# Attention and two MLPs on one core: p·v in two slices instead of four, and the copies of the remaining transposes on ScalarE

## The chip, the core and the metric

The program runs on one core of a Trainium2 chip. The metric is the device time of one execution in microseconds; the time before is the median of 3 runs. The engines are called TensorE (PE in the rows; PEld is its weight load), VectorE (DVE), ScalarE (ACT), GpSimd (POOL) and SyncE (SP, which issues the DMAs).

## The reference

For 4 batches of 8 heads, 576 positions and 64 numbers a head, q and k are turned by a rotary table, softmax attention is taken, and the result goes through two MLPs of width 512 and 2048.

```python
q_rot, k_rot = (rotate(q), rotate(k))
scores = (1.0 / np.sqrt(D)) * np.matmul(q_rot, k_rot.transpose(0, 1, 3, 2))
scores = scores - np.max(scores, axis=-1, keepdims=True)
attn = np.exp(scores)
attn = attn / (np.sum(attn, axis=-1, keepdims=True) + 1e-09)
attn_out = np.matmul(attn, v)
...
h = x @ w_in      # first MLP: 0 below -1, h above 1, (h + 1)**2 / 4 between
x = g @ w_out
...
h = x @ w_in      # second MLP: g = s * max(h, 0)**2 + b
out = g @ w_out
```

## The kernel before

**Units.** Two heads make a pair; 4 batches give 16 pairs. A pair is 9 units: four blocks of 128 query rows for each of the two heads, and one unit for the 64 rows left over from both. Units are numbered n = 0 to 143; the first batch is n = 0 to 35. For each unit `qk` computes the scores `sc` in PSUM on TensorE (L353), VectorE takes the negated row maximum `nm` (L355), and ScalarE the exponential `p` with its row sums (L360). `sc` has two buffers, so the scores of a unit can begin when the exponential of the unit two before has read its own.

**Transposes.** Two units later `tmain` transposes four 128-column blocks of `p` into a PSUM bank `tp` (L375) and copies the bank to `pt`: ScalarE for head 0 and the middle unit (L380, L378), VectorE for head 1 (L382). The last 64 columns of `p` remain. When the units of a group are through, `trem` transposes them (L388, L391) into `tr`, and a copy takes them to `ptr` (L393). A pair has two groups: g = 0 with 320 query rows and g = 1 with 256.

**Products and scaling.** `av` multiplies the transposed `p` by `v`: four key blocks `kt`, each for two heads (L401, two rows of the profile for each product), and then the remaining columns out of `ptr` (L406, L408). These products have 64 columns of weights (128*64 in the rows), the others 128. `inverse` takes the reciprocal of the row sums (L416), which GpSimd spreads into `eb` (L418, one buffer). `finish` runs the products in slices, then transposes `eb` on TensorE into `rm` (L429, L431), copies `rm` to `r` on ScalarE (L434), and multiplies on VectorE (L437 to L440).

**Order.** For n < 48 (`NS`) `finish` yields after each slice, and each slice is issued with the transposes of one unit, beginning three units after the group's last (`LS`). From n = 48 all four blocks go at once, and work of the first MLP fills in between (`run_fill`, L180). GpSimd has the rotary products of the next pair (`qin`, `kin`, L96), and from about 57 us also parts of the weights' conversion (`wm`, `w`). Within the attention a scheduler puts each engine's instructions in order from its own estimate of times, so an edit in one place moves rows on every engine. From about 440 us on, TensorE's order is the order of the code.

Of the kernel before, what the change touches and what calls it, by code (L numbers as in the profile page):

```python
# [24 lines left out]
NP = H // 2  # L25
# [31 lines left out]
NS = 48  # L57
PARK_AT = range(96, 144, 6)
LS = 3
SLICES = [[0], [1], [2], [3]]  # L60
SPLITX = 1
N1 = 288
N7 = 480
# [3 lines left out]
def kernel(ctx, tc, qq, kk, vv, tab, ww1, ww2, s, b, out):  # L67
    nc = tc.nc
# [180 lines left out]
    def bank(name):  # L249
        return ps_b.tile([P, 512], F32, tag="bank", name=name)  # L250
# [86 lines left out]
    pt = {}  # L337
# [46 lines left out]
    def trem(i, g):  # L384

        tp = bank("tr")
        for n in range(2):
            nc.tensor.transpose(tp[:, n * P:(n + 1) * P], p_t.pop((i, 2 * g + n))[:, 512:640], ident)  # L388
        m = 256
        if g == 0:  # L390
            nc.tensor.transpose(tp[:, 256:384], p_t.pop((i, 4))[:, 512:640], ident)  # L391
            m = 384
        nc.vector.tensor_copy(pt["r", g][:, :m], tp[:, :m])  # L393

    def av(i, g, ps, kts):

# [24 lines left out]
    def finish(i, g, e, eb, slices):  # L421
        ps = bank("av")
        for kts in slices:
            av(i, g, ps, kts)
            if 3 not in kts:
                yield
        rm = bank("rm")
        for t in range(2):
            nc.tensor.transpose(rm[:, t * P:(t + 1) * P], eb[:, 2 * t:2 * t + 2, :].rearrange("p j d -> p (j d)"), ident)  # L429
        if g == 0:  # L430
            nc.tensor.transpose(rm[:, 256:384], e[:, 4:5].to_broadcast([P, P]), ident)  # L431
            u_t[i] = att2.tile([P, S], F32, tag="u", name="u")
        r = att2.tile([P, 384], F32, tag="r", name="r", bufs=1)
        nc.scalar.copy(r[:, :384 - 128 * g], rm[:, :384 - 128 * g])  # L434
        u = u_t[i]
        c = slice(256 * g, 256 * g + 256)
        nc.vector.tensor_tensor(out=u[:, c], in0=ps[:, :256], in1=r[:, :256], op=ALU.mult)  # L437
        if g == 0:
            nc.vector.tensor_tensor(out=u[:D, 512:], in0=ps[:D, 256:320], in1=r[:D, 256:320], op=ALU.mult)
            nc.vector.tensor_tensor(out=u[D:, 512:], in0=ps[D:, 256:320], in1=r[D:, 320:384], op=ALU.mult)  # L440
            return
        bb, hp = divmod(i, NP)
        nc.sync.dma_start(out=xd[hp, :, bb * S:(bb + 1) * S], in_=u_t.pop(i))
# [155 lines left out]
    def do_t(n):  # L599
        if LT <= n < len(units) + LT:  # L600
            i, k = units[n - LT]
            tmain(i, k)
            if k in (4, 8):
                trem(i, k // 8)
                rbs[i, k // 8] = inverse(i, k // 8)
# [3 lines left out]
    def do_av(n):  # L609
        late = LS if n < NS else LA  # L610
        for m in range(n - LS if n < NS else n - LA - (n == NS), n - late + 1):
# [3 lines left out]
            if k in (4, 8) and (i, k // 8) in rbs:  # L615
                todo.append((i, k, finish(i, k // 8, *rbs.pop((i, k // 8)), SLICES if n < NS else [range(4)])))
        while todo:
# [561 lines left out]
```

## Time and profile before

| | |
|---|---|
| median of 3 runs | 1115.1 us (1114.06 to 1116.26) |
| the profiled execution | 1114.57 us |
| its span | 1112.8 us |
| TensorE busy | 1074.0 us, 97% of the span |
| VectorE, ScalarE, GpSimd busy | 778.2, 628.5, 431.1 us |
| granted clock | 1.00 over the whole span |

A busy TensorE need not be at its peak: a matmul's row may cover time in which it only passes through, and rows overlap. What the engine's work needs is read from the distance of the starts, or from the chain of work.

### The profile page before, as it was taken

To read this page: it belongs to the slowest core of one execution; us is meant where nothing else is said; L and a number is where in the kernel's file an instruction comes from. 1 tells how busy PE (TensorE), PEld (TensorE's weight loads), DVE (VectorE), ACT (ScalarE), POOL (GpSimd) and SP (SyncE) were. 2 spreads that over 40 slices of the span, in tenths; PEclk is the share of its full clock that TensorE was granted. 3 is DMA by queue.
4 is the path that set the end of the run, shared out by engine and by line. 5 is a ranking of instruction groups with operands and counts; after the bars stand their busy time and mean duration, and the time that the engine had idled before them with its cause. 6 is when DMAs were issued, how large, how long until landed. Compare 5 with 4: busy or idle time off the path is not lost.

```text
span 1112.8 us, 20049 instructions
## 1 busy us (share of the span) xinstructions
PE 1074.0 (97%) x7296; PEld 982.0 (88%) x7296; DVE 778.2 (70%) x1449; ACT 628.5 (56%) x1430; POOL 431.1 (39%) x564
## 2 busy tenths in 40 slices
PE   3999999989999999999999999999999999999998
PEld 3776788877898889999999999999999999999997
DVE  6899988778667653454756667866787778677754
ACT  4777777767666665454545455474555448334431
POOL 7989978686563322432535345110212110000000
PEclk9999999999999999999999999999999999999999
DMA  7665856756675544646465663231322843221221
GB/s 219 172 206 162 260 177 194 226 158 193 195 230 181 159 143 152 224 160 201 136 197 202 212 231 129 67 122 50 124 79 90 313 162 114 83 85 40 81 63 36
DMA packets 109762, 173.24 MB, mean 156 GB/s; under 512 B 29408, under 2 KB 80608, under 8 KB 109664
## 3 DMA queue, kind: packets, MB, share of 16 engines
q1 hardware_dynamic: 109664, 171.97, 48.7%
q8 instruction: 57, 0.93, 0.4%
q14 instruction: 41, 0.34, 0.1%
HBM read 110.10 MB, written 48.56 MB: 143 GB/s over the span
## 4 chain that ended last, share of the span: by engine, by line
PE 82%; DVE 7%; DMA 3%; ACT 3%; POOL 3%; issue 2%; SPq 0%; POOLq 0%; ACTq 0%; DVEq 0%
PE hps L180 15%; PE sum L915 14%; PE yps L831 6%; PE yps L830 6%; PE yps L829 6%; PE y L180 5%; PE sc L353 5%; PE yps L765 4%; PE av L401 4%; PE yps L767 4%; PE yps L766 4%; PE h L180 4%; PE tp L375 3%; DVE nm L355 2%; ACT p L360 1%
## 5 line engine op out<-in xcount | busy, mean ns | idle before, releaser
L180 PE MATMUL hps<-xh,w 128*128 128x288 f32 (+4 forms) x640 | 163.4, 324 | 0.0
L360 ACT ACTIVATE p<-sc,nm 128x576 f32<-128x576 f32 x144 | 106.7, 743 | 32.1 <-DVE nm L355 29.5
L353 PE MATMUL sc<-kh,qs 128*128 128x288 f32 x336 | 103.5, 331 | 22.0 <-DVE qs L307 12.3
L355 DVE TENSOR_REDUCE nm<-sc 128x1 f32<-128x576 f32 x144 | 106.7, 749 | 22.6 <-PE sc L353 21.9
L923 ACT ACTIVATE four<-four,b_sb,s_sb 128x480 f32<-128x480 f32 x64 | 47.4, 783 | 126.3 <-DVE four L922 126.3
L831 PE MATMUL yps<-gh,w 128*128 128x480 f32 (+1 forms) x320 | 118.5, 370 | 0.0
L829 PE MATMUL yps<-gh,w 128*128 128x480 f32 (+1 forms) x320 | 118.4, 370 | 0.0
L830 PE MATMUL yps<-gl,w 128*128 128x480 f32 (+1 forms) x320 | 118.4, 370 | 0.0
L96 POOL TENSOR_TENSOR wm<-wm,w 128x256 f32<-128x256 f32 x80 | 70.0, 896 | 119.1 <-ACT w L138 62.2
L180 PEld LDWEIGHTS hps<-xh,w 128*128 128x128 f32 x640 | 113.3, 188 | 1.0
L180 PE MATMUL hps<-xl,w 128*128 128x288 f32 (+4 forms) x320 | 103.7, 324 | 0.0
L353 PEld LDWEIGHTS sc<-kh,qs 128*128 128x128 f32 x336 | 64.5, 195 | 41.7 <-ACT p L360 20.2
L375 PE MATMUL tp<-ident,p 128*128 128x128 f32 x576 | 88.3, 278 | 6.8 <-ACT p L360 3.3
L353 PE MATMUL sc<-kz,qs 128*128 128x288 f32 x336 | 94.5, 303 | 0.0
L765 PE MATMUL yps<-gh,w 128*128 128x288 f32 (+3 forms) x288 | 93.2, 324 | 1.1 <-ACT ys L503 0.5
L766 PE MATMUL yps<-gl,w 128*128 128x288 f32 (+3 forms) x288 | 92.8, 322 | 0.0
L767 PE MATMUL yps<-gh,w 128*128 128x288 f32 (+3 forms) x288 | 92.8, 322 | 0.0
L96 POOL TENSOR_TENSOR wm<-wm,raw 128x256 f32<-128x256 f32 x16 | 12.8, 819 | 176.5 <-ACT raw L138 176.5
L375 PEld LDWEIGHTS tp<-ident,p 128*128 128x128 f32 x576 | 70.8, 143 | 10.2 <-ACT p L360 3.7
L180 PE MATMUL y<-gh,w 128*128 128x288 f32 x320 | 74.2, 302 | 2.0 <-DVE ptr L393 0.9
L401 PE MATMUL av<-pt,vin 128*64 128x256 f32 (+1 forms) x512 | 75.7, 417 | 0.0
L106 DVE TENSOR_TENSOR gl<-hps,gh 128x288 fp32r<-128x288 f32 (+4 forms) x88 | 46.5, 528 | 40.5 <-ACT gh L102 40.4
(154 smaller groups left out, 2910.3 us busy)
## 6 DMA issues: line engine op xcount, KB each, us to landing
wraw<-in_ww SPq DMA_DIRECT2D x56, 512.0 KB, 4.2
w<-parkd SPq DMA_DIRECT2D x24, 512.0 KB, 6.1
kin<-in_k SPq DMA_DIRECT2D x15, 576.0 KB, 4.8
qin<-in_q SPq DMA_DIRECT2D x15, 576.0 KB, 4.2
kh<-kin SPq DMA_DIRECT2D x60, 144.0 KB, 2.7
parkd<-wraw SPq DMA_DIRECT2D x16, 512.0 KB, 3.3
xs<-y1d SPq DMA_DIRECT2D x32, 240.0 KB, 2.6
xd<-u SPq DMA_DIRECT2D x16, 288.0 KB, 2.7
```

What stands on the lines that cost most here:

```text
L180: m = nc.tensor.matmul(out_ps, l, r, start=(i == 0), stop=(i == n - 1))
L353: nc.tensor.matmul(sc[:, half, o:o + n], l, r[:, k0:k0 + n], start=m == 0, stop=m == len(todo) - 1)
L355: maxs[i * 9 + k] = nc.vector.tensor_reduce(out=nm, in_=sc[:, :, :288], axis=AX.XY, op=ALU.max, negate=True).ins
L375: m = nc.tensor.transpose(v[:, c, :], p[:, c * P:(c + 1) * P], ident)
L401: nc.tensor.matmul(ps[j * D:(j + 1) * D, :n], v[:, kt, j, :], pt[g][:, kt, j, :], start=kt == 0, stop=False)
L765: nc.tensor.matmul(acc, wh, gh, start=f == 0, stop=False)
L766: nc.tensor.matmul(acc, wh, gl, start=False, stop=False)
L767: nc.tensor.matmul(acc, wl, gh, start=False, stop=last)
L829: nc.tensor.matmul(acc, wh, gh, start=f == 0, stop=False)
L830: nc.tensor.matmul(acc, wh, gl, start=False, stop=False)
L831: nc.tensor.matmul(acc, wl, gh, start=False, stop=last)
L915: nc.tensor.matmul(acc, l, r, start=j == 0, stop=j == len(t) - 1)
```

## The change

Each group of the first 48 units now runs its products in two slices of two key blocks, so the last slice stands two units earlier; and for the four pairs of the first batch (i < `NP`, which is 4) ScalarE copies `tr` to `ptr`, not VectorE.

```diff
-SLICES = [[0], [1], [2], [3]]
+SLICES = [[0, 1], [2, 3]]
...
-        nc.vector.tensor_copy(pt["r", g][:, :m], tp[:, :m])
+        (nc.scalar.copy if i < NP else nc.vector.tensor_copy)(pt["r", g][:, :m], tp[:, :m])
```

On TensorE, at the first group of the first pair, from the transposes ahead of its first slice, there stood before (x2 are the two heads of one key block):

```order
L375 MATMUL tp<-ident,p 128x128 x4
L401 MATMUL av<-pt,vin 64x320 x2
L353 MATMUL sc<-kh,qs_107 128x288
L353 MATMUL sc<-kz_109,qs_107 128x288
L353 MATMUL sc<-kh,qs_107 128x288
L353 MATMUL sc<-kz_109,qs_107 128x288
L375 MATMUL tp<-ident,p 128x128 x4
L401 MATMUL av<-pt,vin 64x320 x2
```

and there stands now:

```order
L375 MATMUL tp<-ident,p 128x128 x4
L401 MATMUL av<-pt,vin 64x320 x4
L353 MATMUL sc<-kh,qs_107 128x288
L353 MATMUL sc<-kz_109,qs_107 128x288
L353 MATMUL sc<-kh,qs_107 128x288
L353 MATMUL sc<-kz_109,qs_107 128x288
L375 MATMUL tp<-ident,p 128x128 x4
L401 MATMUL av<-pt,vin 64x320 x4
L406 MATMUL av<-ptr,vin 64x64 x2
L408 MATMUL av<-ptr,vin 64x256 x2
L429 MATMUL rm<-ident,eb 128x128 x2
```

Four products follow each other where two did, and the remaining products and the `rm` transposes come after the second slice instead of the fourth. Over the whole program TensorE goes over from other work to products of 64 weight columns 61 times before and 43 times now.

On ScalarE, in the third group (pair 1, first group), the copy now stands behind that of the middle unit (`pt` of L378):

```order
L360 ACTIVATE p,sums<-sc,nm 128x576
L378 COPY pt<-tp 128x8x64
L393 COPY ptr<-tr 128x384
L306 ACTIVATE qs_108<-qin 64x576
L360 ACTIVATE p,sums<-sc,nm 128x576
```

So a copy and the scaling of `qs` lie there between two exponentials.

On GpSimd, the ninth group's `eb` (pair 4, first group) stood before in this place, behind the memset of `vin`:

```order
L96 TENSOR_TENSOR w<-wm,wa 128x256 x2
L96 TENSOR_TENSOR kin<-kin,tab_sb 128x2x144 x4
L274 MEMSET vin 64x64
L418 COPY eb<-sume 128x256
L96 TENSOR_TENSOR kin<-kin 128x288
```

and now it stands here:

```order
L96 TENSOR_TENSOR kin<-kin,tab_sb 128x2x144 x2
L96 TENSOR_TENSOR wm<-wm,w 128x256 x2
L274 MEMSET vin 64x64
L96 TENSOR_TENSOR kin<-kin 128x288 x2
L418 COPY eb<-sume 128x256
```

Two pieces of `wm` and two of `kin` are now ahead of it. The `eb` of the fifth group came behind one more piece of `kin` and one of `w`, that of the seventh behind one more piece of `kin`.

## Rows read from the trace of the kernel before

**Rows 1.** Windows: length; busy PE, PEld, DVE, ACT, POOL; clock, DMA share, GB/s.
```profile
25.13:52.65 27.52, 27.52 (x185) 21.45 (x184) 23.62 (x38) 21.11 (x50) 26.35 (x33) 1.00 0.62 173
52.65:75.00 22.35, 21.85 (x159) 15.49 (x158) 21.15 (x34) 17.39 (x42) 19.54 (x25) 1.00 0.61 172
75.00:92.00 17.00, 16.85 (x125) 11.73 (x123) 15.21 (x27) 12.99 (x31) 14.20 (x19) 1.00 0.63 189
92.00:130.00 38.00, 34.91 (x254) 25.28 (x254) 36.04 (x60) 29.34 (x71) 35.37 (x46) 1.00 0.76 227
55.79:74.14 18.35, 18.35 (x136) 13.22 (x135) 17.24 (x30) 13.93 (x34) 15.86 (x21) 1.00 0.61 178
```

**Rows 2.** TensorE's waits, 130 to 450: first and last of ten (us, times, longest).
```profile
PE sc L353 <- ACT p L360: 3.9, 6, 1.4
...
PE tr L388 <- ACT ys L503: 0.3, 1, 0.3
```

**Rows 3.** TensorE's waits, 450 to the end: first of two rows.
```profile
PE yps L765 <- ACT ys L503: 0.5, 1, 0.5
```

**Rows 4.** Chain that ended last, 30 to 53: start, us, what.
```profile
36.56 0.69 PE av L401 x4
37.25 0.72 PE sc L353 x4
...
41.32 0.53 PE sc L353 x4
41.85 0.58 PE av L401 x4
```

**Rows 5.** The same chain, 128 to 200.
```profile
184.43 2.30 PE av L401 x16
...
197.06 1.88 PE av L401 x16
```

**Rows 6.** Lines by form, 25.13 to 92: count, busy us, mean ns, idle before.
```profile
L393 DVE COPY ptr<-tr 128x384 f32<-128x384 f32 x4 | 2.2, 546 | 0.0
...
L434 ACT COPY r<-rm 128x384 f32<-128x384 f32 x3 | 1.4, 480 | 0.7 <-PE rm L431 0.7
...
L393 DVE COPY ptr<-tr 128x256 f32<-128x256 f32 x3 | 1.2, 414 | 0.0
...
L434 ACT COPY r<-rm 128x256 f32<-128x256 f32 x3 | 1.1, 366 | 0.2 <-PE rm L429 0.2
```

**Rows 7.** Timeline of GpSimd: start, us, instruction.
```profile
70.92 0.39 POOL L418 COPY eb<-sume 128x256 f32<-128x256 f32 x1
...
83.20 1.92 POOL L96 TENSOR_TENSOR wm<-wm,w 128x256 f32<-128x256 f32 x2
...
89.57 0.85 POOL L418 COPY eb<-sume 128x256 f32<-128x256 f32 x1
...
107.76 0.39 POOL L418 COPY eb<-sume 128x256 f32<-128x256 f32 x1
```

**Rows 8.** Timeline of TensorE, the rm transposes of three groups.
```profile
76.41 0.44 PE L429 MATMUL rm<-ident,eb 128*128 128x128 f32 x2
...
94.89 0.44 PE L429 MATMUL rm<-ident,eb 128*128 128x128 f32 x2
...
115.00 0.44 PE L429 MATMUL rm<-ident,eb 128*128 128x128 f32 x2
```

**Rows 9.** GpSimd's waits, 25.13 to 92.
```profile
POOL qin L96 <- DMA qin<-in_q: 3.0, 2, 2.4
POOL eb L418 <- PE rm L429: 2.6, 2, 2.4
```

**Rows 10.** Timeline of ScalarE: a PSUM copy and two exponentials.
```profile
68.25 0.60 ACT L378 COPY pt<-tp 128x512 f32<-128x512 f32 x1
68.73 0.77 ACT L360 ACTIVATE p<-sc,nm 128x576 f32<-128x576 f32 x1
...
87.50 0.74 ACT L360 ACTIVATE p<-sc,nm 128x576 f32<-128x576 f32 x1 [0.63 <-DVE nm L355]
```

## The prediction

> **What bounds the kernel now.** I read the windows by stage first, because the edit touches the first 48 units alone, which are through at about 120 us. After 25 us TensorE is nearly always busy: 27.52 of 27.52 us, 21.85 of 22.35 and 16.85 of 17.00 [rows 1]. That is 66.22 of 66.87 us, with VectorE at 59.98, ScalarE at 51.49 and GpSimd at 60.09. From 92 to 130 it turns round: VectorE is busy for 36.04 of 38.00 us, and TensorE stands for 3.1. A busy TensorE can hide waits, so I then read the chain of work from 30 to 53 us: it runs on TensorE from row to row, transposes, products, scores [rows 4]. For the later stages I read the waits of TensorE: the largest from 130 to 450 us is 3.9 us, the smallest shown 0.3, and all ten add up to 11.7 [rows 2]; from 450 us to the end the two together are 0.9 [rows 3]. So an early microsecond won on TensorE should still be there at the end, because behind it TensorE goes on nearly without a gap.
>
> **Breaks on TensorE, removed.** Going over to the products and back costs time. Four rows of products take 0.69 us and sixteen in one piece 2.30 [rows 4, 5], so a row inside costs (2.30 - 0.69)/12 = 0.134 us and the entry 0.69 - 4 x 0.134 = 0.15. For 256 columns 0.58 and 1.88 give 0.108 a row and again 0.15. Scores behind products take 0.72 us, behind transposes 0.53 [rows 4], so the way back costs 0.19. A break is thus worth 0.34 us. The order on TensorE has 18 fewer of them over the program. Two go in each group, and the first six groups, which lie whole before 92 us, lose twelve: 12 x 0.34 = 4.1 us. The others fall after 92 us, where TensorE waits for VectorE anyway; I give them nothing, and at most 6 x 0.34 = 2.0 more.
>
> **Copies off VectorE.** From 25 to 92 us there are seven of the eight copies, four of 546 ns and three of 414 [rows 6], 3.4 us together. Does the first term need them? After it the stretch would last 66.87 - 4.1 = 62.8 us. VectorE without the copies has 59.98 - 3.4 = 56.6 to do, 90% of it, the share that it has now (59.98/66.87). With them it would be at 96%. So the second edit adds nothing of its own to the sum: it lets the first arrive. Without it, at a share of 90%, the stretch could not shorten at all, and at 96% by the whole 4.1 us; halfway is 2 us.
>
> **Copies onto ScalarE.** ScalarE's copies of the same shapes out of PSUM, those of `r`, take 480 and 366 ns [rows 6]. Eight copies are 4 x 0.48 + 4 x 0.37 = 3.4 us more on an engine with 15.4 us idle in the stretch. The price is what stands behind one in the queue: an exponential, and behind that TensorE's next scores. In one place the exponential starts without a wait behind the copy of `pt` (68.25, then 68.73), and there a further copy delays it in full; at 87.50 it waited 0.63 us for the maximum, and there the copy hides [rows 10]. Between nothing and 3.4 us I take a quarter, 0.8, since about half stand in such a place and TensorE has other work ready for part of that.
>
> **`rm` two units earlier.** A unit takes 18.35/9 = 2.04 us [rows 1], so TensorE now wants `eb` 4.1 us earlier, and everything behind `rm` in its queue (the scores of the next unit) waits if GpSimd has it not ready. Margins now: fifth group, `eb` done at 70.92 + 0.39 = 71.31, `rm` at 76.41, so 5.1 us; seventh 94.89 - 90.42 = 4.5; ninth 115.00 - 108.15 = 6.85 [rows 7, 8]. Take off 4.1, and the pieces that the new order puts ahead of `eb`: 0.96 us each by the `wm` rows (1.92 for two) [rows 7], two for the fifth group, one for the seventh, four for the ninth. That leaves -0.9, -0.6 and -1.1 us. Against this GpSimd itself waited 2.6 us for `rm` of the group before, since `eb` has one buffer [rows 9], and gets that back. I charge 0.9 us for one such wait; the ends are nothing and, with ten groups at 1 us, 10 us.
>
> **GpSimd as a lid.** It was busy for 60.09 us of 66.87. Of the 6.8 idle us 2.6 go, as just said. If the other 4.2 (3.0 of them for the loading of `qin` [rows 9]) stay as they are, it cannot pass the stretch under 64.3 us, so that 2.6 us is the most the stretch can gain, where the other terms give 4.1 - 0.8 - 0.9 = 2.4. The two agree nearly, and I keep 2.4.
>
> **Behind 130 us** the scheduler puts rows in another order on all engines, though the work is the same. I set this at nothing; its bounds are about half of the 11.7 us of waits either way.
>
> **Sum.** 1114.57 - 2.4 = 1112.2 us for the profiled execution. It is 0.5 us under the median of the three runs, so against that median I forecast 1115.1 - 2.4 = **1112.7 us**. What a measurement here tells from no change is about 0.2%, 2.2 us, so the forecast lies just beyond that edge.
>
> **Rivals.**
> - *VectorE alone is the bound, and breaks are worth nothing.* For it: GpSimd and VectorE share the load closely, and from 55.79 to 74.14 TensorE's weight load is busy for only 13.22 of 18.35 us, 72%, while VectorE is at 94% [rows 1]. Then only the copies behind 52.65 us count, two of 546 and three of 414 ns, 2.3 us, less the 0.8 and 0.9 from above: 1114.5 us, no change. Against it: the same window has TensorE busy for all of its 18.35 us, and the starts in the chain show no gap for what would be headroom. The Trainium skill (Perfetto Trace Analysis, "Identifying the Most-Contended Engine") says to judge TensorE by its weight load's share and not by its matmuls' busy time, and by that rule VectorE would be the engine to relieve, and the breaks would give nothing. The chain [rows 4] does not bear it out. Chance 0.2.
> - *`eb` comes late, and TensorE stands.* GpSimd's in-order queue at 90% is what speaks for it. It makes the kernel slower than before by over 2.2 us once the ten groups lose 4.1 - 0.8 + 2.2 = 5.5 us, 0.55 us each. At 0.8 us each, 8 us in all, the sum is +4.7: 1119.8 us. Against it: the first, third, fourth, sixth and eighth groups keep more room, and TensorE's order puts some `rm` behind the next scores. Chance 0.1.
> - *The later order is worse.* If the waits between 130 and 450 us grow by 5 us, the time is 1117.7. Nothing in the profile speaks for it but that every engine's order changes. Chance 0.1.
> - *Everything fits.* GpSimd's loads come earlier too, the copies hide, and the last groups' breaks or the later order give some 2 us: 1115.1 - 6 = 1109 us. Chance 0.12.
>
> **Numbers.** The forecast's own case, a gain of 1.3 to 4 us, has 0.48, and about two thirds of it lie beyond 2.2 us. Faster: 0.32 + 0.12 = 0.44. The same: 0.16 and the first rival's 0.2, 0.36 together. Slower: the second and third, 0.2. For 8 in 10 the range goes from the case where everything fits, 1109, to the third rival, 1117.7, and leaves out the late `eb` in its dear form and some of what lies below. Its own range for the likeliest case is 1111 to 1114.
>
> **What would show it.** Right: the same units pass from 25 to 92 us in 64 to 65 us, products stand as eight rows in the chain with one entry, TensorE stays nearly gapless there, and from 450 us on all is shifted by one amount. Wrong: TensorE's waits show `rm` behind GpSimd; waits of the scores for the exponential grow by more than a microsecond; VectorE's idle time grows by what the copies gave back; or the shift at 130 us is gone by 450, which would put the cause into the later order.

## The result, and the profile after

The changed kernel takes 1120.85 us (median of 5 runs, 1119.31 to 1122.18), the kernel before beside it 1115.25 (1114.06 to 1116.26): a ratio of 1.0051 [1.0038, 1.0064], 5.6 us slower. The forecast was 1112.7 us with a range up to 1117.7. The profiled execution took 1119.31 us, its span 1117.5, 4.7 more than before.

The windows of the changed kernel over the same stretches as [rows 1] (length; busy PE, PEld, DVE, ACT, POOL; clock, DMA share, GB/s):

```profile
25.13:52.65 27.52, 24.64 (x180) 18.58 (x179) 21.81 (x33) 20.82 (x51) 23.82 (x31) 1.00 0.64 178
52.65:75.00 22.35, 18.86 (x146) 14.46 (x148) 17.75 (x27) 16.54 (x40) 20.03 (x26) 1.00 0.55 153
75.00:92.00 17.00, 15.96 (x122) 12.05 (x118) 14.22 (x26) 12.93 (x32) 13.22 (x19) 1.00 0.69 198
92.00:130.00 38.00, 32.43 (x243) 24.67 (x242) 34.53 (x56) 28.23 (x68) 33.61 (x42) 1.00 0.71 206
```

TensorE was busy for 66.22 of 66.87 us from 25 to 92; now it is for 59.46. But VectorE is less busy too (53.78 where it was 59.98), and so are the other two: nobody took the room. What TensorE waits for shows it. First its waits from 25 to 130 us in the kernel before, then in the changed kernel (us, times, longest):

```profile
PE sc L353 <- ACT p L360: 3.6, 5, 1.2
```

```profile
PE sc L353 <- ACT p L360: 11.7, 13, 2.4
PE av L401 <- DVE pt L382: 1.2, 2, 0.6
```

The scores wait for the exponential that has to read their buffer first, that of the unit two before: 8 us more. Behind 130 us the list adds up to 12.0 us over nine rows against 11.7 [rows 2], and from 450 us on one row of 0.5 is left [rows 3]:

```profile
PE sc L353 <- ACT p L360: 5.5, 8, 1.5
PE y L180 <- DVE gl L106: 1.5, 2, 1.1
...
```

To compare the same work and not the same clock time, I cut windows by units: from the start of the exponential of unit 2 to that of unit 50, in three pieces of 16 units, and read the sum line. Before, then after:

```profile
sum 101.86, PE 98.40 PEld 71.85 DVE 93.31 ACT 77.87 POOL 91.29; mean PE 32.80 PEld 23.95 DVE 31.10 ACT 25.96 POOL 30.43
```

```profile
sum 106.64, PE 93.23 PEld 70.70 DVE 90.19 ACT 80.30 POOL 91.00; mean PE 31.08 PEld 23.57 DVE 30.06 ACT 26.77 POOL 30.33
```

TensorE's busy time fell by 5.2 us, and its idle time rose from 3.5 to 13.4, at a granted clock of 1.00 in all pieces of both. The three pieces got 3.8, 0.5 and 0.5 us longer; in the second and third TensorE is busy for 2.3 and 2.7 us less, and idle for 2.9 and 3.2 more.

The following table is the tool for all that comes: the start of a unit's exponential in ScalarE's timeline, less the same start in the kernel before (us). The versions are explained with the experiments. Unit 4 shows what is only the beginning of the program; units 48 to 66 what the attention of the first units brought; 140 is behind all of the first MLP's filling. Each row is one profiled execution, which need not be the typical one: that of "products halved" took 2.1 us more than the median of its kernel, that of "room on VectorE, four" 1.9.

| kernel | 4 | 16 | 18 | 36 | 48 | 50 | 66 | 84 | 104 | 140 |
|---|---|---|---|---|---|---|---|---|---|---|
| changed | -0.7 | -0.3 | +3.1 | +4.9 | +3.1 | +4.1 | +5.3 | +6.3 | +5.9 | +5.9 |
| slices only | -0.5 | -0.2 | +2.7 | +5.2 | +6.4 | +6.5 | +7.1 | +12.4 | +9.6 | +10.0 |
| copies only | -0.3 | -1.1 | -1.0 | -1.1 | -1.7 | -1.8 | -1.7 | -1.8 | -0.1 | -0.1 |
| k load first | -0.4 | -0.0 | +1.2 | +7.4 | +5.2 | +4.3 | +12.9 | +17.0 | +13.9 | +14.0 |
| k load behind v | -0.5 | -0.6 | -1.4 | +3.8 | +4.3 | +2.7 | +4.8 | +9.0 | +9.1 | +9.4 |
| two slices, spread | -0.4 | -1.0 | -0.2 | +3.5 | +2.8 | +1.2 | +3.2 | +2.8 | +2.9 | +3.0 |
| three slices | -0.5 | -1.3 | -0.4 | +0.6 | +2.1 | +1.4 | +4.4 | +4.9 | +1.0 | +5.0 |
| code order, four | +0.7 | +1.8 | +1.7 | +5.1 | +3.5 | +3.0 | +17.8 | +21.6 | +18.9 | +24.1 |
| code order, two | +0.8 | -0.1 | +2.9 | +4.7 | +3.3 | +3.7 | +17.5 | +18.5 | +16.9 | +20.4 |
| room on VectorE, four | -0.7 | -0.7 | -0.7 | -0.6 | -2.1 | -4.1 | -0.1 | +3.1 | +2.9 | +3.0 |
| room on VectorE, two | -0.3 | +0.0 | +3.5 | +4.4 | +2.4 | +0.9 | +2.0 | +5.5 | +1.6 | +1.7 |
| room on VectorE, spread | -0.3 | -1.5 | -1.2 | +0.7 | -2.8 | -2.3 | -1.3 | +3.1 | -2.1 | -2.0 |
| rm apart, copies | -0.5 | -1.2 | -1.0 | -1.1 | -1.0 | -1.9 | -1.6 | +5.7 | +5.9 | +6.0 |
| one head left out | -0.6 | -0.6 | -0.6 | -0.9 | -2.6 | -3.7 | -1.7 | +10.3 | +7.9 | +8.0 |
| one head left out, two | -0.5 | -0.7 | +0.8 | +5.4 | +5.1 | +4.9 | +5.8 | +11.3 | +10.1 | +10.3 |
| products halved | -0.4 | -1.1 | -1.4 | -2.2 | -5.2 | -6.5 | -6.9 | +5.1 | +6.8 | +6.9 |
| k not multiplied, four | -1.3 | -2.5 | -2.7 | +0.3 | -1.1 | -1.8 | +0.8 | +1.5 | -1.4 | +1.9 |
| k not multiplied, two | -1.8 | +0.3 | +1.5 | +7.9 | +6.4 | +7.8 | +10.5 | +16.0 | +14.7 | +14.7 |
| both | -1.3 | -2.9 | -2.8 | -0.2 | -1.0 | -2.3 | -1.5 | +1.5 | +2.3 | +2.4 |

The changed kernel loses 3.4 us between units 16 and 18, holds that with some swing to unit 48, and has 4.1 at unit 50. At 130 us, between units 52 and 53 of the kernel before, the shift is 4.2 to 4.8 us. It goes up to 5.9 by unit 104, 1.2 us of that come back by 630 us for a reason that stays open, and the end is 4.7 us late. So the loss arises before 130 us; what comes behind moves it to and fro.

**The step at unit 18.** The chain of work that ended last, in the changed kernel:

```profile
40.95 0.61 DVE pt L382
...
41.60 1.08 PE av L401 x6
42.67 0.73 PE sc L353 x4
43.41 0.44 PE tp L375 x4
43.84 1.01 PE av L401 x8
...
45.33 0.60 SPq L268
...
48.03 0.53 SPq L443
...
48.67 5.06 DMA kin<-in_k
...
53.94 3.66 POOL kin L96 x5
...
58.25 0.80 POOL kin L96
...
59.08 0.67 ACT kin L318
59.75 0.74 ACT p L360 x2
...
60.53 0.81 PE sc L353 x4
```

The products are through earlier, which frees a buffer of `vin`, so SyncE's queue now has the loads of the third pair's v ahead of the fifth pair's k. In SyncE's own timeline, before and then after:

```profile
46.07 0.33 SPq L261 DMA_DIRECT2D kin<-in_k  x1
48.28 1.95 SPq L268 DMA_DIRECT2D vin<-in_v  x3
```

```profile
45.33 2.61 SPq L268 DMA_DIRECT2D vin<-in_v  x4
48.03 0.53 SPq L443 DMA_DIRECT2D xd<-u  x1
48.67 0.43 SPq L261 DMA_DIRECT2D kin<-in_k  x1
```

The load goes out 2.6 us later, GpSimd waits for it, ScalarE's conversion of `kin` waits for GpSimd, and the exponential stands behind that conversion in ScalarE's queue. No row of the prediction was about SyncE.

### The profile page after: what moved, and what is told of

It is laid out like the page before. It is cut to its first block, busy times and chain, and to the rows that moved or that the text cites. A ratio compares the mean times of both kernels' runs of the same rounds, so it can differ in the third digit from the quotient of the medians.

```text
span 1117.5 us, 20060 instructions
## 1 busy us (share of the span) xinstructions
PE 1070.3 (96%) x7296; PEld 983.4 (88%) x7296; DVE 776.3 (69%) x1441; ACT 631.2 (56%) x1438; POOL 430.3 (39%) x564
## 4 chain that ended last, share of the span: by engine, by line
PE 79%; DVE 7%; DMA 5%; POOL 3%; ACT 3%; issue 2%; SPq 1%; POOLq 0%; ACTq 0%; DVEq 0%
PE hps L180 15%; PE sum L915 13%; PE yps L831 6%; PE yps L830 6%; PE yps L829 6%; PE sc L353 4%; PE yps L765 4%; PE y L180 4%; PE yps L767 4%; PE yps L766 4%; PE h L180 4%; PE av L401 3%; PE tp L375 3%; DMA qin<-in_q 1%; POOL qin L96 1%
## 5 line engine op out<-in xcount | busy, mean ns | idle before, releaser
L180 PE MATMUL h<-xh,w 128*128 128x288 f32 x320 | 72.0, 301 | 4.1 <-ACT ys L503 1.1
```

The costliest lines, as they stand in the source:

```text
L180: m = nc.tensor.matmul(out_ps, l, r, start=(i == 0), stop=(i == n - 1))
```

## The experiments

The theories, as they came up. **Queue (Q):** the k load behind the v loads is the loss. **Bursts (B):** two heavy units with four products each are followed by two or three light ones without; with two score buffers TensorE cannot work ahead in the light ones, so it idles there for what it saved in the heavy ones. **Copies (C):** the copies on ScalarE delay exponentials. **Order:** every edit shifts rows on all engines, and the kernel before lies well. Later also **VectorE as a lid** and **GpSimd as a lid**.

### First: the parts, and the queue

Slices only (the copies back on VectorE) and copies only (`SLICES` as before) undo one half of the diff each. The other two force the order on SyncE:

```diff
# k load first: the changed kernel, with the v loads of pair 2 behind the k load of pair 4
...
+                if n == 20:
+                    load_qk(4, "q")
+                    with tc.issue_after(load_qk(4, "k")):
+                        load_v(2)
# k load behind v: the kernel before
...
-                    load_qk(i + 2, "q" if k == 4 else "k")
+                    with tc.issue_after(vdma[2]) if (i, k) == (2, 6) else ExitStack():
+                        load_qk(i + 2, "q" if k == 4 else "k")
```

Slices only: 

> Two slices, but the copies of the remaining transposes stay on VectorE. Theory Q (the queue): with products done earlier, SyncE's order puts the loads of v ahead of a later pair's load of k; that load comes some 3 us late, GpSimd waits for it, a cast on ScalarE waits for GpSimd, and the exponential behind it and TensorE's scores wait too. The order of this kernel has the loads of v ahead as the changed kernel has, so Q expects +3 to +6 us against the kernel before. Theory B (bursts): eight products in a row hold up the next scores, and with two score buffers the lighter units in between can't make up for it; it expects +3 to +6 us too. Theory C (the copies on ScalarE delay the exponentials): no copies are moved, so -1 to +1 us.

Copies only: 

> Four slices as before, the copies of the first batch on ScalarE. The order of SyncE is the same as before, that of TensorE nearly. Q and B expect -1.5 to +1 us against the kernel before; C expects +3 to +6 us.

k load first: 

> The changed kernel (two slices, copies on ScalarE), with one order forced on SyncE: the fifth pair's load of k stands ahead of the third pair's loads of v, as it did in the kernel before. Q expects the step at the 18th unit to go, and +1 to +3 us against the kernel before instead of +5.6. B and C expect +4.5 to +6 us, since the slices and the copies are those of the changed kernel.

k load behind v: 

> The kernel before (four slices, copies on VectorE), with the opposite order forced on SyncE: the fifth pair's load of k stands behind the third pair's loads of v, as in the changed kernel. Q expects +2 to +4 us against the kernel before, with GpSimd waiting for that load; less if the scheduler, which knows of the order, moves the cast on ScalarE out of the way. B and C expect -1 to +1 us.

Measured: slices only 1123.45 us, ratio 1.0076 [1.0060, 1.0092]; copies only 1114.15, 0.9987 [0.9977, 0.9997]; k load first 1129.28, 1.0125 [1.0107, 1.0144]; k load behind v 1122.54, 1.0068 [1.0053, 1.0084].

The slices cost, the copies do not: C has fallen. Slices only, k load first and k load behind v all lie outside what any theory had expected, on the slow side. Copies only is the one version which leaves no work out that is faster than the kernel before, by 1.4 us, barely more than its interval. It was 1.5 us ahead up to unit 84 (-1.8, less the -0.3 of the beginning) and lost that between units 84 and 104; its windows there:

```profile
230.00:235.00 5.00, 3.44 (x17) 3.21 (x18) 3.95 (x10) 3.91 (x11) 5.00 (x9) 0.69 0.31 105
235.00:240.00 5.00, 5.00 (x28) 4.98 (x27) 1.68 (x4) 3.69 (x9) 3.48 (x4) 0.62 0.11 30
```

Of Q the place is right and the sum wrong. With the k load forced behind the v loads, GpSimd waits 6.7 us in one place (for the transfer of `kin` to `kh`), and the kernel before loses 5.2 us between units 18 and 36. Put ahead of them, it takes the step at unit 18 down from 3.4 to 1.2 us, and the kernel then loses 6.2 between units 18 and 36. So the step is real, but it is not all that the change costs. Part of the losses behind it can be the clock's: behind the v loads it was 0.50 from 66 to 68 us, with the k load first from 71 to 73, in slices only from 110 to 113; the changed kernel had 1.00 throughout these units.

### Second: the bursts by themselves

```diff
-SLICES = [[0, 1], [2, 3]]
+SLICES = [[0, 1], [], [2, 3]]        (two slices, spread)
+SLICES = [[0, 1], [2], [3]]          (three slices)
-M1 = False
+M1 = True                            (TensorE in code order; four slices, and two)
```

Spread and three slices keep the copies on ScalarE, and in both the k load stands ahead of the v loads. In code order, TensorE's rows stand as the program has them, and not as the scheduler put them.

Spread: 

> The changed kernel with an empty slice between its two slices, so that a unit with four products is followed by one without, and the rm transposes come one unit later. The order of the engines keeps the fifth pair's k load ahead of the third pair's v loads, as in the kernel before. Bursts (TensorE cannot run ahead of two score buffers, so it idles in a unit without products what it lost in one with four): the unit without products now lies between the two heavy ones, and part of the lulls goes; with the queue's 3 us gone as well, 1114 to 1117 us, the exponential of unit 20 within 1 us of the kernel before, and TensorE's waits for ACT p from 25 to 130 us at 5 to 9 us. Order (any edit here moves the rows of all engines, and the kernel before had a lucky order): 1118 to 1124 us, with the loss in steps at places that have nothing to do with the units of four products. No theory makes it faster than 1113 us.

Three: 

> The changed kernel with three slices: four products in the first unit, two in each of the next two; one break less a group than before instead of two. The k load stays ahead of the v loads here too. Bursts: the load is smoother than in two slices; half of the break savings (2 us of 4) are at stake and half of the lulls come with them, 1114 to 1117 us. Order: 1118 to 1124 us, in steps that lie elsewhere.

Code order, four slices: 

> The kernel before with TensorE in the order of the code from the first instruction on, where the scheduler chose it before; the other engines are still scheduled. It is there as the partner of the next. All theories: 1125 to 1190 us, since the filling work of the first MLP stands where the code put it.

Code order, two slices: 

> The changed kernel with TensorE in the order of the code, so that against its partner TensorE's order differs in the slices alone. The k load is behind the v loads here as in the changed kernel. Bursts: against its partner the first 16 units gain nothing although 0.34 us a break are saved, TensorE's waits for ACT p grow by as much as the breaks gave, and with the queue's step at unit 18 it is 2 to 6 us slower than its partner. Order: with TensorE's order fixed the breaks saved (4 us) come through, at most the queue's 3 us go against them, and it is within 2 us of its partner or faster.

Measured: spread 1116.86 us, ratio 1.0019 [1.0010, 1.0028]; three slices 1118.90, 1.0034 [1.0022, 1.0047]; code order 1135.33 with four slices and 1137.42 with two (ranges 1134.91 to 1140.57 and 1133.29 to 1138.90, so no difference).

At unit 48 the versions stand as the bunching would have it: copies only -1.7, three slices +2.1, spread +2.8, the changed kernel +3.1. But this last has the queue's step of 3.4 us in it, and without it the order would be another. TensorE's idle time between units 2 and 50 is 2.5, 7.6, 7.4 and 13.4 us in these four. The pair in code order fits less well: two slices are 1.8 us ahead of four at unit 16, where B wanted nothing, lose 3.0 at the queue's step, win 1.4 again, and are level at unit 48 (-0.2). By the whole time the pair fits Order's expectation (within 2 us, or faster), but TensorE's waits for exponentials from 25 to 130 us grew as B wanted, from 6.4 to 11.8 us. The whole time of three slices lies where Order wanted it, beyond B's range; 2.9 us of that arose between units 48 and 140.

TensorE's timelines show the bursts more directly. Take its idle time between units 2 and 50, behind the first product, and count what follows twelve or more rows of scores and transposes without a product, so a light stretch. In the kernel before that is 0.8 us, in the changed kernel 10.1 us in ten places, 2.4 of them at the queue's step. In all seven kernels of this document with two slices it is 8.2 to 13.6 us, in all ten with four at most 1.8; three slices have 5.7, spread 4.9 (1.6 with room on VectorE). In code order, where the scheduler has no hand in TensorE's rows, it is 0.0 us with four slices and 9.7 with two. So this idle time comes with the slices, whatever the order. One such place in the changed kernel, on TensorE, then on VectorE:

```profile
107.65 0.60 PE L375 MATMUL tp<-ident,p 128*128 128x128 f32 x4
109.81 0.40 PE L353 MATMUL sc<-kh,qs 128*128 128x288 f32 x1 [1.55 <-ACT p L360]
```

```profile
106.93 0.41 DVE L437 TENSOR_TENSOR u<-av,r 128x256 f32<-128x256 f32 x1
107.26 0.96 DVE L137 SCALAR_TENSOR_TENSOR wa<-wraw,wa 128x512 f32<-128x512 uint16 x1
108.14 0.75 DVE L355 TENSOR_REDUCE nm<-sc 128x1 f32<-128x576 f32 x1
```

Here the exponential waits for its maximum, and VectorE comes to that without a pause from the scaling and a conversion. In four of the ten places, 5.6 us together, the exponential waited for a maximum before which VectorE had no pause: part of the light units' slowness is VectorE's queue.

### Third: room on VectorE

```diff
+            if lean[0]:
+                nc.scalar.copy(hi, a)
+                pool_tt(out=m, in0=a, in1=hi, op=ALU.subtract)
+                pool_tt(out=lo, in0=m, in1=a, op=ALU.add)
+                return
```

These kernels leave out VectorE's part (L134 to L137) of the weights' conversions, so those weights are not right; `lean` holds for the conversions that the first 51 steps issue. A fourth version goes the other way from two slices: four slices, the copies on ScalarE, and `rm` in a step of its own.

Four slices: 

> The kernel before, with the four VectorE instructions (wm and wa, L134 to L137) of the weights' conversions left out that the attention's first 51 steps issue; so the values of those weights are not computed rightly, and GpSimd and ScalarE keep their part. VectorE has some 15 us less to do between 55 and 130 us. It is the partner of the next two. If VectorE is the lid behind 55 us, unit 48 starts 3 to 8 us earlier than in the kernel before; if GpSimd or the order of rows is, 0 to 2 us. In all 1104 to 1115 us.

Two slices: 

> The changed kernel with the same VectorE instructions left out. Its k load is still behind the v loads. VectorE as a lid (it has to be fed all the time from 55 us on, and a lull in TensorE's bursts is lost for good): with room on VectorE the loss against its partner shrinks from 3 to 5 us at units 36 and 48 to between 0 and 2, and what is left is the queue's step at unit 18. Order (every edit shifts rows, and the kernel before lies well by luck): the loss stays at 3 to 7 us.

Two slices, spread: 

> The version with an empty slice between the two, with the same VectorE instructions left out; its k load is ahead of the v loads. VectorE as a lid: the savings of the breaks come through now, and at units 36 and 48 it is 1 to 4 us ahead of its partner, where with the conversions it was 3.5 and 2.8 us behind. Order: it stays 2 to 4 us behind.

rm apart: 

> Four slices as before, the copies on ScalarE, and the rm transposes in a step of their own one unit after the fourth slice, so that the heaviest unit gets lighter: the opposite way to two slices. If bursts on TensorE and the feeding of VectorE are the cause, it is at or under the version with the copies alone (1114.2): 1111 to 1114 us. Order: 1114 to 1121 us.

Measured: 1115.83, 1114.32 and 1111.78 us (ratios 1.0010 [1.0000, 1.0020], 0.9997 [0.9986, 1.0007], 0.9972 [0.9960, 0.9983]); rm apart 1121.41, 1.0066 [1.0047, 1.0084].

By the whole times VectorE as a lid looks confirmed; by the units it is one in the last piece alone. With 14 us less on VectorE between units 2 and 50 (78.96 against 93.31) the partner with four slices starts unit 48 2.1 us earlier than the kernel before (0.7 of it already at unit 4), and unit 50 4.1 us earlier. The pieces from unit 18 to 34 and from 34 to 50, in the kernel before and then in this partner:

```profile
56.57:89.27 32.70, 32.55 (x243) 23.53 (x242) 29.83 (x52) 24.91 (x59) 27.31 (x35) 1.00 0.63 189
89.27:125.70 36.43, 34.06 (x248) 24.21 (x245) 34.74 (x56) 27.77 (x67) 33.88 (x44) 1.00 0.73 214
```

```profile
55.88:88.52 32.64, 32.48 (x243) 23.46 (x242) 24.82 (x44) 26.02 (x62) 25.69 (x36) 1.00 0.64 201
88.52:121.61 33.09, 32.32 (x239) 22.99 (x237) 25.37 (x43) 26.59 (x66) 31.32 (x46) 1.00 0.75 227
```

5.0 us less on VectorE give nothing in the first of these, and 9.4 less give 3.3 us in the second. Of the loss by the slices these conversions are not the cause: two slices are 4.6 us behind their partner at unit 48, where they were 3.1 behind without the room. Spread is level with its partner (-0.7) where 1 to 4 us ahead were wanted. The whole times come out in this order because the partner lost 5 us between units 48 and 104, and two slices did not. rm apart tells the same from the other side: -1.0 at unit 48, 0.7 behind copies only, and +5.9 at 104; its whole time lies beyond what both theories wanted.

### Fourth: TensorE's time taken away evenly

```diff
# one head left out
+                if i < 5 and (kt, j) in ((1, 1), (2, 0)):
+                    continue
# products halved
+                m = n // 2 if i < 5 and kt in (1, 2) else n
-                nc.tensor.matmul(ps[j * D:(j + 1) * D, :n], v[:, kt, j, :], pt[g][:, kt, j, :], start=kt == 0, stop=False)
+                nc.tensor.matmul(ps[j * D:(j + 1) * D, :m], v[:, kt, j, :], pt[g][:, kt, j, :m], start=kt == 0, stop=False)
# k not multiplied by the rotary table
+            if nm == "q" or i > 5:
                 tt[mul](out=t[:, :, c], in0=t[:, :, c], in1=tab_sb[:, :, c], op=ALU.mult)
```

One head left out, four slices: 

> The kernel before with two of the eight products of p with v left out in each group of the first five pairs (head 1 of the second key block, head 0 of the third), so the outputs of these heads lack those terms. Each of the second and third slice loses two rows; by four rows of 0.134 us in a first group and four of 0.108 in a second, five of each, TensorE has 4.8 us less to do, about what the breaks would have saved, but spread evenly, and no break, no DMA and no row of the first 320 moves otherwise. If TensorE's time is the bound of this stretch, unit 48 starts 3 to 5 us earlier than in the kernel before: then the breaks' saving was real and the bunching of the products lost it. If the bound is elsewhere (the loop from scores to maximum, exponential and scores again with two buffers, VectorE or GpSimd), unit 48 starts within 1.5 us of before, and TensorE's idle time grows by 3 us or more: then the saving had no worth here from the start. The whole time then lies within 5 us of before either way, since the order behind unit 52 moves it.

One head left out, two slices: 

> The changed kernel with the same products left out. If TensorE's time is the bound in its heavy units, unit 48 starts 2 to 5 us earlier than in the changed kernel; if the bound is elsewhere, within 1.5 us of it. Its k load stays behind the v loads, and the step at unit 18 stays, 2.5 to 4.5 us against the kernel without products left out in four slices.

Products halved: 

> The kernel before with the products of the second and third key block narrowed to half their columns in the first five pairs (both heads), so the other columns lack those two blocks. The run that left out one of two heads took no time off TensorE (two rows took 0.68 us where four took 0.69), so this one shortens both heads' rows alike: four rows by 0.067 us in a first group, by 0.054 in a second, two slices each, five groups of each: 4.8 us less, spread evenly, no break and no DMA moved. If TensorE's time is the bound of the first 48 units, unit 48 starts 3 to 5 us earlier than in the kernel before. If the loop of loads, GpSimd's rotary products, VectorE and ScalarE is, within 1.5 us of before.

k not multiplied, four slices: 

> The kernel before without the multiplication of k by the rotary table in pairs 1 to 5 (the addition behind it stays), so k is not turned in these. GpSimd has four rows of about 1 us less a pair, some 20 us less by unit 48. If GpSimd's rotary chain sets the pace, unit 48 starts 4 us or more earlier than in the kernel before, down to where TensorE binds. If not, within 1.5 us.

k not multiplied, two slices: 

> The changed kernel with the same multiplications of k left out; here the k load stands ahead of the v loads. If GpSimd's chain is what kept the saving of the breaks from showing, it is 2 to 4 us ahead of its partner without those multiplications at unit 48. If the bunching of the products loses it (two score buffers), it stays 1 to 5 us behind its partner.

Both: 

> Four slices, the multiplications of k left out and the products of two key blocks narrowed to half as well. If GpSimd is the bound and TensorE the next, unit 48 starts 3 to 5 us earlier than in the version with the k multiplications left out alone. If TensorE is the bound by itself, that holds with the multiplications too (the narrowed version against the kernel before). If neither, within 1.5 us.

Measured: 1123.23 us, ratio 1.0073 [1.0060, 1.0086]; 1123.11, 1.0068 [1.0052, 1.0083]; halved 1119.24, 1.0037 [1.0024, 1.0051]; k not multiplied 1115.01, 0.9999 [0.9988, 1.0010]; with two slices 1128.62, 1.0121 [1.0106, 1.0136]; both 1115.65, 1.0008 [0.9997, 1.0019].

Leaving out one head took nothing off TensorE, so it tested nothing. The chain of that kernel shows it, with four rows of products and then with two:

```profile
32.26 0.69 PE av L403 x4
...
34.12 0.68 PE av L403 x2
```

Its units moved all the same: it stands at -2.6 at unit 48, and with two slices 2.0 us behind the changed kernel, the first between the two expectations, the second outside both. So an edit can move the units by two microseconds with nothing taken off TensorE.

Halving the columns for both heads did take time off. The sum line between units 2 and 50:

```profile
sum 95.85, PE 92.30 PEld 70.90 DVE 87.75 ACT 76.36 POOL 85.77; mean PE 30.77 PEld 23.63 DVE 29.25 ACT 25.45 POOL 28.59
```

Unit 48 starts 5.2 us earlier than before, 4.8 after the beginning's 0.4, and 4.8 is what was to be taken away. That this agrees is in part luck. By the distance of the starts the narrowed slices took 1.5, 1.4 and 1.5 us less in the three pieces, and the pieces got 0.9, 1.0 and 4.1 us shorter. In the last one VectorE has 4.4 us less to do as well, since conversions moved behind unit 50; one head left out, which saved nothing, shortened it by 2.8, with VectorE relieved by as much. So from unit 2 to 34 about two thirds of TensorE's time taken away came through, and in the last piece its share cannot be told. Idle time stayed at 3.6 us where the changed kernel, with as much saved, has 13.4.

GpSimd is no lid: 14.7 us less on it (76.62 against 91.29) left unit 48 where it was (-1.1, and -1.3 already at unit 4), though the three pieces changed by -1.4, +2.9 and -2.0 us on the way. With k not multiplied, two slices have the k load ahead and GpSimd at ease, and are still 7.5 us behind four at unit 48. The mean clock from unit 2 to 34 was 0.95 there and 1.00 in the partner, over 73.7 us, so by an estimate up to 3.7 us of this are the clock's; the rest is a loss without the queue's step, as B has it. The version with both edits is level with its partner at unit 48, the outcome that the expectation put down to neither GpSimd nor TensorE. Its clock was 0.95 from unit 34 to 50 (36.6 us, so up to 1.8 us), which does not make up the 3 to 5 us; this run stays against TensorE as the only bound.

**What became of 6.9 us.** The halved version is 6.9 us ahead at unit 66 and 1.7 behind at unit 70. Its windows, waits of TensorE from 155 to 200 us, and chain there:

```profile
160.00:165.00 5.00, 5.00 (x40) 4.85 (x38) 2.54 (x5) 3.13 (x9) 3.10 (x5) 1.00 0.86 316
165.00:170.00 5.00, 1.41 (x5) 0.98 (x4) 4.62 (x6) 2.19 (x4) 5.00 (x7) 0.74 0.01 2
170.00:175.00 5.00, 3.35 (x14) 2.43 (x16) 1.87 (x4) 2.45 (x5) 4.22 (x6) 0.50 0.86 219
```

```profile
PE sc L353 <- ACT p L360: 3.4, 2, 2.9
PE y L180 <- POOL w L96: 2.4, 1, 2.4
```

```profile
164.19 0.81 POOL qin L96
165.00 1.88 POOL wm L96 x2
166.88 3.52 POOL kin L96 x4
170.40 1.21 POOL w L96
...
171.65 1.54 PE y L180 x4
```

TensorE reaches the first MLP's products before GpSimd has their weights (`w`): GpSimd works through `qin`, `wm` and `kin` without a pause, TensorE stands, and then its clock is at the lower of its two levels, 1.2 GHz, for all of 170 to 175 us. The versions that were ahead at unit 66 lost most up to unit 140: halved 13.8 us, one head left out 9.7, rm apart 7.5, copies only 1.7; the changed kernel, 5.3 behind at unit 66, lost 0.5. It is no rule: spread with room on VectorE was 1.3 ahead and lost nothing, and k load behind v, 4.8 behind, lost 4.6.

## Why the prediction was wrong

**What bounds the kernel: right where the runs can tell.** From unit 18 to 34 TensorE is idle for 0.15 of 32.70 us, 5.0 us less on VectorE change nothing, and two thirds of the time taken away evenly up to unit 34 came through. Behind that VectorE bounds too (3.3 us came back when it was relieved), as the prediction read from [rows 1]. The first rival, VectorE alone, fell with that. The Trainium skill (Perfetto Trace Analysis, "Identifying the Most-Contended Engine") judges TensorE by the share of its weight load; that was 23.53 of 32.70 us from unit 18 to 34, so by it there was headroom, and VectorE was ahead with 29.83. That relieving VectorE gave nothing there speaks against it.

**Breaks, 4.1 us: the size was right, the step to the time failed.** Eight rows in one piece take 1.23 us in the chain of the changed kernel where two pieces of four took 0.69 each [rows 4], and TensorE's busy time fell by 5.2 us between units 2 and 50. But the term counted every break as time won, 12 x 0.34, as if only the sum of TensorE's work mattered. This is the step that failed. The change also bunches this work. As B has it, the others wait for TensorE in a heavy unit; in a light one TensorE waits for the exponential, since it has two score buffers and no more. The idle time went from 3.5 to 13.4 us, most of it in light stretches: 10.1 us where there were 0.8. The prediction itself had named as a sign of being wrong that "waits of the scores for the exponential grow by more than a microsecond"; they grew by 8. Between units 2 and 50, 5.2 us less work and 9.9 more idle time made the kernel 4.8 us longer, 2.4 of the idle time at the queue's step. That the bunching makes this idle time is shown by its place: 8.2 us or more of it in every kernel with two slices, 1.8 or less in every one with four. How much of it is the two buffers and how much VectorE's queue, and how much of each version's loss is the new order of rows beside it, the runs do not separate: two slices against their partners came out at unit 48 between level (code order) and 7.7 us behind (one head left out, with a clock of 0.50 from 89 to 92 us).

**Copies off VectorE, no own gain; copies onto ScalarE, -0.8: the second too dear, the first too low.** Alone, they left the waits for exponentials as they were (3.1 us in TensorE's list) and gained 1.5 us by unit 48.

**`rm` earlier, -0.9, and GpSimd as a lid, 2.6: neither as put.** No row shows TensorE waiting for `eb`, and GpSimd relieved of 14.7 us changed nothing by unit 48. What was moved and not counted is behind `rm`: the scaling (L437 to L440) also comes earlier on VectorE, and the loads and the store of `u` that the finished products release come earlier on SyncE. This second one is the 3.4 us at unit 18.

**"Behind 130 us", set at nothing: right in size for this change, wrong in its reason.** The shift was 4.2 to 4.8 us at 130 us and 4.7 at the end, well within the bounds of half of 11.7. So the third rival, a worse later order, is not what happened. The second, with 1119.8 us, came nearest in time, but no row shows its cause, a wait for `eb`. And "an early microsecond won on TensorE should still be there at the end" does not hold: the kernels' shift between units 66 and 140 moved by up to 13.8 us. The waits of TensorE [rows 2] show what it waited for at its old pace. They do not show what stood ready just in time: 6.9 us earlier, the weights are not there.

## What to carry to other kernels

A saving on the bounding engine counts only if the work beside it keeps its rhythm: before summing prices, write down what a unit needs from each engine before and after, and look how far the engine may run ahead (here two score buffers). When work is finished earlier, follow what it releases, the loads in SyncE's queue above all. And a gain early in the program is worth at the end only what the later stages have ready earlier: look for what arrives just in time, not only for waits.

## What the runs showed of the hardware

**Two products side by side.** Two rows of products with 64 weight columns took 0.68 us where four took 0.69. The two heads write to different halves of the output's partitions, and leaving out one of them saves nothing. The Trainium skill (TensorE: Matmul & The Clock Gate, "Why this matters for your kernels") says that small matmuls whose outputs go to different partition groups run at the same time; the trace agrees. So the prediction's 0.134 us for a row is a price only for two rows side by side, 0.27 us together.

**The clock after a lull.** Where TensorE was busy for 1.41 of 5 us (165 to 170 us, products halved), the clock was 0.50 in the next 5 us; in the copies-only version it was 0.69 and 0.62 from 230 to 240 us. In its profile the kernel before kept 1.00 in the same place, though TensorE was busy for less:

```profile
230.00:235.00 5.00, 2.67 (x20) 2.19 (x19) 4.86 (x10) 3.86 (x13) 4.87 (x8) 1.00 0.29 107
```

So a similar lull can cost or not. Copies only lost 1.7 us between units 84 and 104; the lower clock in its two stretches can account for that by an estimate (0.31 and 0.38 of 5 us, so 3.5 us at most).
